# A sparse-attention and two-MoE kernel: other turns for the first six weight decodes, uneven MoE steps in eight turns, earlier first weight load, and a late mask on VectorE

## The chip, the cores and the metric

The kernel runs on one core of a Trainium2 chip. The metric is device time in microseconds (us) of one execution; lower is better. Before the change the median of three runs is 950.56 us (949.97 to 950.58).

## The reference

Four batches of eight heads, 576 positions, 64 dimensions per head. The first four heads see the last 32 positions (local), the other four see every 32nd position (strided). The result goes through two dense feed-forward stages:

```python
scores = scale * q @ k.T
scores = where(mask, scores, -1e9)          # local heads: 0 <= i-j < 32; strided: i >= j, i%32 == j%32
attn = softmax(scores) @ v                  # [4, 8, 576, 64] -> x [2304, 512]
x = (sigmoid(x @ w_gate) * (x @ w_val)) @ w_out        # 512 -> 1536 -> 512
x = (relu(h) + log1p(exp(-abs(h)))) @ moe2_w_out       # h = x @ moe2_w_in, 512 -> 2048 -> 512
```

All of it is float32, and the weights arrive as 64-bit floats.

## The kernel before

**Precision.** A feed-forward product is made of three fp32r matmuls (`mm3`, lines 67 to 69: high x high, high x low, low x high), each with 512 moving columns. So every activation and every weight exists as a high and a low part (`xh`/`xl`, `w..h`/`w..l`, `gh`/`gl`).

**Weights.** They arrive as raw 64-bit words in pieces of 512 KB (`load_next`, line 97, three buffers `raw`), issued on SP. A piece is decoded by `decode_steps`: on VectorE (DVE) lines 108, 112, 117, 122 and, in the attention part, 125; on ScalarE (ACT) line 121; on GpSimd (POOL) line 126. Each decode writes one half of one weight tile. The first six pieces are the gate, value and output weights of the first feed-forward group, two pieces each.

**Attention in turns.** The 32 units (batch, pair of heads, first or second half) run in a software pipeline of 35 turns. Turn `u` (function `stage`) emits, in this order: the exponential of unit u-1 (ACT); the scores of unit u (PE), their row maximum and the subtraction (DVE, lines 435 and 436); loads; the values product of unit u-3 (PE, line 485, `ps_o`); the first half of a decode; then the row sum and reciprocal of unit u-1 (DVE, 451 and 452) with the scaling on POOL (453); the second half of the decode; the output of unit u-3 (`xh` on ACT 505, `xl` on DVE 506); then the transposes of unit u-2 (PE, 467, in two pieces) with their copies to `pt` on ACT (470). The order of emission is the order on each engine. So ACT's copy `pt` of a turn stands behind that turn's decode, the transposes of unit u-2 wait for POOL's scaling of the turn before, and the second transposes of a turn take over a PSUM buffer that `xl` (DVE) of the turn before has to release.

**The mask.** It is added on PE: a matmul of an identity (`one`) with a broadcast mask table (`m_loc`, `m_str`) opens the accumulation (line 422), and the score matmuls (429) add to it. The identity, both tables and the zeros in the two q buffers (`qbuf`) are written at the start by POOL and DVE.

**Feed-forward steps between.** `window(0)` is the first group on the first 512 tokens: 8 gate steps, 8 value steps, 8 output steps, each of three matmuls. Six gate steps run in turns 7, 8 and 9 (`ahead`); the other 18 are spread over turns 11 to 18 (`t == 0`) as 2, 2, 2, 3, 2, 2, 2, 3. Turns 19 to 26 hold 64 steps and turns 27 to 34 hold 48. Gate steps need `xl`/`xh` of the head pair that they read, value steps need decodes 3 and 4, output steps need decodes 5 and 6 and the split products `gh`, `gl`.

**Decodes.** `decode_at` lists the turns with a decode: 4, 5, 9, 10, 12, 13, then 18 to 23. `load_next` runs at the start, in turns 2, 5, 6, 7, and after each decode from turn 8 on.

**Warm-ups.** `keep_busy(n)` issues n matmuls of 512 columns whose result (`ps_w`) nobody reads: three at the start and one in each of turns 0 to 8.

After the attention part some 760 us of feed-forward matmuls follow, which the change doesn't touch.

Of the kernel before, what the change touches and what calls it, by code (L numbers as in the profile page):

```python
# [8 lines left out]
F32 = mybir.dt.float32  # L9
# [4 lines left out]
ALU = mybir.AluOpType  # L14
# [6 lines left out]
P = 128  # L21
# [11 lines left out]
HQ = 64  # L33
# [10 lines left out]
def tile_sparse_attention_moe_moe2(  # L44
# [10 lines left out]
    nc = tc.nc  # L55
# [36 lines left out]
    def load_next():  # L92
        if todo:
            g, m, c = piece = todo.pop(0)
            src = w1[g, m] if g < NG1 else w2[g - NG1, m // 2]
            raw = rawp.tile([P, PIECE], U64, tag="raw", name="raw")
            nc.sync.dma_start(out=raw, in_=src[:, c * PIECE:(c + 1) * PIECE])
            raws[piece] = raw
            queue.append(piece)

    def decode_steps(pools, refill=True):
        g, m, c = piece = queue.pop(0)
        words = raws.pop(piece).bitcast(U32).rearrange("p (n t) -> p n t", t=2)
        low, high = words[:, :, 0], words[:, :, 1]
        hi, lo = (x[:, c * PIECE:(c + 1) * PIECE] for x in wset[g % 2][m])
        f = pools["d"].tile([P, PIECE], U32, tag="f", name="f")
        e = pools["d"].tile([P, PIECE], U32, tag="e", name="e")
        nc.vector.tensor_scalar(
            out=f, in0=high, scalar1=3, scalar2=0x3FFFFFFF,
            op0=ALU.logical_shift_left, op1=ALU.bitwise_and,  # L110
        )
        nc.vector.scalar_tensor_tensor(  # L112
            out=f, in0=high, scalar=0xC0000000, in1=f,
            op0=ALU.bitwise_and, op1=ALU.bitwise_or,
        )
        yield
        nc.vector.tensor_scalar(
            out=e, in0=f, scalar1=0xFF800000, scalar2=None, op0=ALU.bitwise_and
        )
        ff, ef = f.bitcast(F32), e.bitcast(F32)  # L120
        nc.scalar.activation(out=hi, in_=ff, func=AF.Copy)  # L121
        nc.vector.scalar_tensor_tensor(
            out=ef, in0=low, scalar=2.0 ** -52, in1=ef, op0=ALU.mult, op1=ALU.mult
        )
        pools["e"].tensor_tensor(out=ff, in0=ff, in1=hi.bitcast(F32), op=ALU.subtract)  # L125
        nc.gpsimd.tensor_tensor(out=lo, in0=ff, in1=ef, op=ALU.add)
        if refill:
            load_next()
        yield
# [151 lines left out]
    def attention():  # L281
        with ExitStack() as actx:
# [29 lines left out]
            qbuf = [const.tile([P, 2, QW], F32, name=f"qbuf{j}") for j in range(2)]  # L312

            def load(j, parts=1):
                b, hp, c0, cn = units[2 * j]
                loc, w, m = dims(2 * j)
                cn += units[2 * j + 1][3]
                qq = qbuf[j % 2]
                kk = qkp.tile([P, STRIDE + S], F32, tag="k", name="kt")
                k0, kn = (0, STRIDE + S) if loc else (STRIDE, cn * m)  # L320
                qn = (cn - 1) * m + HQ
                for i in range(parts):
                    for h in range(2):
                        r = slice(h * HQ, (h + 1) * HQ)
                        a, e = (0, units[0][3] * m, qn)[i:i + 2] if parts > 1 else (0, qn)
                        nc.sync.dma_start(out=qq[r, h, a:e], in_=q[b, hp][r, a:e])
                    a, e = (0, units[0][3] * m + w - m, kn)[i:i + 2] if parts > 1 else (0, kn)
                    (nc.scalar if j < 2 else nc.sync).dma_start(
                        out=kk[:, a:e], in_=k[b, hp][:, k0 + a:k0 + e]
                    )  # L330
                for i in (2 * j, 2 * j + 1):
                    qt[i], kt[i] = qq, kk

# [9 lines left out]
            load(1)  # L343
            load_v(0)
            load_v(1)
            load_next()
            load_v(2)

            scratch = acc[NBA - 1]
            ident = scratch[:, 0:P]  # L350
            make_identity(nc, ident)
            nc.vector.memset(qbuf[0][HQ:2 * HQ, 0, :], 0.0)
            nc.vector.memset(qbuf[0][0:HQ, 1, :], 0.0)

            one = const.tile([P, P], F32R, name="one")
            nc.vector.tensor_copy(one, ident)
# [5 lines left out]

            for t in sbuf:
                nc.vector.memset(t[:, :, LK:], 1e-9)
            for t in qbuf[1:]:
                nc.vector.memset(t[HQ:2 * HQ, 0, :], 0.0)
                nc.vector.memset(t[0:HQ, 1, :], 0.0)

# [33 lines left out]
            def mask_runs(i):  # L402
                b, hp, c0, cn = units[i]
                if hp >= NLP:
                    return [(0, cn, m_str)]
                first, rest = m_loc[:, 0:LK], m_loc[:, LK:2 * LK]
                return [(0, 1, first), (1, cn, rest)] if c0 == 0 else [(0, cn, rest)]
# [3 lines left out]
            def scores(i):  # L411
                b, hp, c0, cn = units[i]
                loc, w, m = dims(i)
                qq, kk = qt.pop(i), kt.pop(i)
                s = sbuf[i % 3][:, 0:cn, LK - w:LK]
                st = smp.tile([P, 2, 6], F32, tag="st", name="st")
                sm[i] = (s, sbuf[i % 3][:, 0:cn, LK - w:], st)
                ps = ps_s.tile([P, TB], F32, tag="s", name="ps_s")
                pv = ps[:, 0:cn * w].rearrange("p (c w) -> p c w", c=cn)
                runs = mask_runs(i)  # L420
                for j, (a0, a1, t) in enumerate(runs):
                    nc.tensor.matmul(
                        pv[:, a0:a1, :], lhsT=one,
                        rhs=t.unsqueeze(1).to_broadcast([P, a1 - a0, w]),
                        start=(j == 0), stop=False,
                    )
                for c in range(cn):
                    for h in range(2):
                        nc.tensor.matmul(  # L429
                            pv[h * HQ:(h + 1) * HQ, c, :],  # L430
                            lhsT=qq[:, h, (c0 + c) * m:(c0 + c) * m + HQ],
                            rhs=kk[:, (c0 + c) * m:(c0 + c) * m + w], start=False, stop=(c == cn - 1),
                        )
                top = st[:, 0, 0:cn]
                nc.vector.tensor_reduce(out=top, in_=pv, axis=AX.X, op=ALU.max)
                nc.vector.tensor_tensor(
                    out=s, in0=pv, in1=top.unsqueeze(2).to_broadcast([P, cn, w]), op=ALU.subtract
                )
# [73 lines left out]
            START = PB + SKEW  # L512

            def stage(u):
                dec = decode_steps(pools, u >= PB) if u in decode_at else iter(())
                if 0 <= u - 1 < NU:
                    exponent(u - 1)
                if u < NU:
                    scores(u)
                if u % 2 and u + 3 < NU:  # L520
                    load((u + 3) // 2)
                if 0 <= u - 3 < NU:
                    values(u - 3)
                if 3 <= u < NU:
                    load_v(u)
                if u in (2, 5, 6, 7):
                    load_next()
                next(dec, None)
                yield
                if 0 <= u - 1 < NU:  # L530
                    normalize(u - 1)
                next(dec, None)
                if 0 <= u - 3 < NU:
                    outputs(u - 3)
                yield
                if 0 <= u - 2 < NU:
                    yield from p_transposes(u - 2)
# [11 lines left out]
                    yield from step((0, 2), (1, 2), pools)  # L549

            ahead = {START - 4: 2, START - 3: 2, START - 2: 2}
            units_of = [3 * GC * NCC, 8 * GC * NCC, 6 * GC * NCC]
            units_of[0] -= sum(ahead.values())
            filler = window(0)
            decode_at = (4, 5, 9, 10, 12, 13) + tuple(range(18, 24))
            keep_busy(3)
            for u in range(NU + SKEW):
                t, pos = divmod(u - START, PB)
                if t > 0 and pos == 0:
                    for _ in filler:  # L560
                        pass
                    filler = window(t)
                fill = ahead.get(u, 0)
                if t >= 0:
                    total = units_of[t]
                    fill = (pos + 1) * total // PB - pos * total // PB
                n = 0
                for j, _ in enumerate(stage(u)):
                    if u < START - 2 and j == 1:
                        keep_busy(1)  # L570
                    while n < fill * (j + 1) // 4:
                        n += 1
                        next(filler, None)
                while n < fill:
                    n += 1
                    next(filler, None)
# [3 lines left out]
    with tc.manual_schedule():  # L580
# [12 lines left out]
        for i, cur in enumerate(rest):  # L593
            g, t = cur
# [91 lines left out]
```

## Time and profile before

| | before |
|---|---|
| median of three runs | 950.56 us |
| the profiled execution's own time | 950.28 us |
| its span in the profile | 948.5 us |
| PE busy | 931.4 us (98%) |
| DVE busy | 601.8 us (63%) |
| ACT busy | 383.9 us (40%) |
| POOL busy | 229.3 us (24%) |

A busy share is over the whole span. The stages differ: the first 71 us are attention with few feed-forward steps, up to about 190 us both run together, after that there is feed-forward work alone. The busy time of PE is modelled for pipelined matmuls, so PE reads as busy also at half clock; PEclk, the granted share of 2.4 GHz, is read beside it.

### The profile page before, as it was taken

Reading aid. Unit: us, or ns where it says so; the run is one execution under the profiler, and the core shown is the slowest. Engines: PE = TensorE matmul, PEld = TensorE weight load, DVE = VectorE, ACT = ScalarE, POOL = GpSimd, SP = SyncE. Lnnn points to the kernel's source line nnn. Section 1 sums busy time; section 2 is a strip of 40 time slices with the busy share of each in tenths; the row PEclk is TensorE's granted clock in tenths of the full one; section 3 lists DMA queues with packets and bytes.
Section 4 is the critical chain, followed back from the end, with each engine's and each line's share of the span. In section 5 each row is a group of like instructions: output and inputs, shape, how many; then the busy total and the mean of one; then the engine's idle time right before and its main releaser. Section 6 shows DMA issues by size and latency. Waiting matters only on the chain.

```text
span 948.5 us, 13659 instructions
## 1 busy us (share of the span) xinstructions
PE 931.4 (98%) x5476; PEld 776.3 (82%) x5476; DVE 601.8 (63%) x979; ACT 383.9 (40%) x693; POOL 229.3 (24%) x194
## 2 busy tenths in 40 slices
PE   7889999999999999999999999999999999999998
PEld 5667888789888888888888887888888888888886
DVE  7787765337567367457555467676767685858554
ACT  2455545524122112112123355454545554545443
POOL 3232211004224023122125442221313040403000
PEclk9889999999999999999999999999999999999999
DMA  8655332002112011011110011110101020200022
GB/s 226 186 159 154 122 101 61 17 1 89 45 45 81 8 45 67 23 45 46 45 37 30 22 45 45 36 53 23 67 23 66 6 85 1 82 8 23 0 89 112
DMA packets 20688, 57.44 MB, mean 61 GB/s; under 512 B 2704, under 2 KB 3216, under 8 KB 20624
## 3 DMA queue, kind: packets, MB, share of 16 engines
q1 hardware_dynamic: 20192, 55.94, 18.3%
q8 instruction: 43, 0.70, 0.3%
q10 hardware_dynamic: 432, 0.62, 0.2%
q14 instruction: 21, 0.17, 0.1%
HBM read 51.83 MB, written 4.72 MB: 60 GB/s over the span
## 4 chain that ended last, share of the span: by engine, by line
PE 92%; DVE 5%; ACT 1%; POOL 1%; issue 1%; POOLq 0%; DVEq 0%
PE ps_y L67 12%; PE ps_y L69 12%; PE ps_y L68 12%; PE ps_h L69 7%; PE ps_h L68 7%; PE ps_h L67 7%; PE ps_g L67 5%; PE ps_g L68 5%; PE ps_g L69 5%; PE ps_v L67 5%; PE ps_v L69 5%; PE ps_v L68 5%; PE ps_s L429 2%; PE ps_o L485 2%; PE ps_p L467 1%; DVE f L112 1%
## 5 line engine op out<-in xcount | busy, mean ns | idle before, releaser
L156 ACT ACTIVATE gh<-sg 128x512 fp32r<-128x512 f32 (+1 forms) x140 | 82.5, 589 | 255.0 <-DVE sg L189 183.8
L157 DVE TENSOR_TENSOR gl<-sg,gh 128x512 fp32r<-128x512 f32 (+1 forms) x140 | 98.7, 705 | 50.2 <-ACT gh L156 46.6
L260 DVE TENSOR_TENSOR acc<-ps_y,acc 128x512 f32<-128x512 f32 x126 | 86.6, 688 | 68.4 <-PE ps_y L69 66.8
L209 DVE TENSOR_TENSOR acc<-ps_y,acc 128x512 f32<-128x512 f32 (+1 forms) x100 | 61.5, 634 | 68.7 <-PE ps_y L69 68.6
L240 DVE SCALAR_TENSOR_TENSOR sg<-ps_h,sg 128x512 f32<-128x512 f32 (+1 forms) x80 | 50.5, 632 | 37.2 <-ACT sg L233 37.1
L189 DVE TENSOR_TENSOR sg<-ps_v,sg 128x512 f32<-128x512 f32 (+1 forms) x60 | 38.2, 636 | 56.2 <-PE ps_v L69 56.1
L231 ACT ACTIVATE sg<-ps_h 128x512 f32<-128x512 f32 (+1 forms) x80 | 43.8, 548 | 61.2 <-PE ps_h L69 61.2
L112 DVE SCALAR_TENSOR_TENSOR f<-raw,f 128x512 uint32<-128x512 uint32 x68 | 66.4, 977 | 2.3
L125 POOL TENSOR_TENSOR f<-f,w00h 128x512 f32<-128x512 f32 x12 | 18.5, 1544 | 184.6 <-ACT w00h L121 184.6
L68 PE MATMUL ps_h<-xl,w00h 128*128 128x512 f32 (+1 forms) x160 | 58.9, 368 | 0.0
L69 PE MATMUL ps_h<-xh,w00l 128*128 128x512 f32 (+1 forms) x160 | 58.8, 368 | 0.0
L69 PE MATMUL ps_h<-xh,w10l 128*128 128x512 f32 (+1 forms) x160 | 58.8, 368 | 0.0
L68 PE MATMUL ps_h<-xl,w10h 128*128 128x512 f32 (+1 forms) x160 | 58.8, 368 | 0.0
L67 PE MATMUL ps_h<-xh,w00h 128*128 128x512 f32 (+1 forms) x160 | 58.8, 368 | 0.0
L67 PE MATMUL ps_h<-xh,w10h 128*128 128x512 f32 (+1 forms) x160 | 58.8, 368 | 0.0
L67 PE MATMUL ps_y<-w02h,gh 128*128 128x512 f32 x144 | 56.2, 391 | 0.6 <-ACT gh L156 0.6
L68 PE MATMUL ps_y<-w02l,gh 128*128 128x512 f32 x144 | 56.1, 390 | 0.0
L67 PE MATMUL ps_y<-w12h,gh 128*128 128x512 f32 x144 | 56.1, 390 | 0.0
L69 PE MATMUL ps_y<-w02h,gl 128*128 128x512 f32 x144 | 56.1, 390 | 0.0
L68 PE MATMUL ps_y<-w12l,gh 128*128 128x512 f32 x144 | 56.1, 390 | 0.0
L69 PE MATMUL ps_y<-w12h,gl 128*128 128x512 f32 x144 | 56.1, 390 | 0.0
L453 POOL TENSOR_TENSOR sm<-sm,st 128x480 f32<-128x480 f32 (+3 forms) x32 | 25.6, 799 | 123.9 <-DVE st L452 85.7
(121 smaller groups left out, 2420.6 us busy)
## 6 DMA issues: line engine op xcount, KB each, us to landing
raw<-in_w_dram SPq DMA_DIRECT2D x68, 512.0 KB, 3.4
out_dram<-acc SPq DMA_DIRECT2D x18, 256.0 KB, 2.0
qbuf<-in_q_dram SPq DMA_DIRECT2D x16, 151.0 KB, 3.5
kt<-in_k_dram SPq DMA_DIRECT2D x8, 297.0 KB, 4.0
qbuf<-in_q_dram SPq DMA_DIRECT2D x14, 144.0 KB, 3.6
vt<-in_vl_dram SPq DMA_DIRECT2D x8, 240.0 KB, 3.1
kt<-in_k_dram SPq DMA_DIRECT2D x6, 304.0 KB, 4.2
vt<-in_vl_dram SPq DMA_DIRECT2D x8, 192.0 KB, 3.8
```

The costliest lines, as they stand in the source:

```text
L67: nc.tensor.matmul(ps, lhsT=lh, rhs=rh, start=first, stop=False)
L68: nc.tensor.matmul(ps, lhsT=lh, rhs=rl, start=False, stop=False)
L69: nc.tensor.matmul(ps, lhsT=ll, rhs=rh, start=False, stop=last)
L112: nc.vector.scalar_tensor_tensor(out=f, in0=high, scalar=0xC0000000, in1=f, op0=ALU.bitwise_and, op1=ALU.bitwise_or,)
L156: nc.scalar.activation(out=gh[:, c, 0:n], in_=src, func=AF.Copy)
L157: nc.vector.tensor_tensor(out=gl[:, c, 0:n], in0=src, in1=gh[:, c, 0:n].bitcast(F32), op=ALU.subtract)
L189: nc.vector.tensor_tensor(out=sg, in0=ps[:, 0:n], in1=sg, op=ALU.mult)
L209: nc.vector.tensor_tensor(out=y, in0=ps[:, 0:n], in1=y, op=ALU.add)
L231: nc.scalar.activation(out=sg, in_=ps, func=AF.Abs)
L240: nc.vector.scalar_tensor_tensor(out=sg, in0=ps, scalar=0.0, in1=sg, op0=ALU.max, op1=ALU.add)
L260: nc.vector.tensor_tensor(out=y, in0=ps, in1=y, op=ALU.add)
L453: nc.gpsimd.tensor_tensor(out=s[:m2], in0=s[:m2], in1=r.unsqueeze(2).to_broadcast([m2, cn, w]), op=ALU.mult,)
```

## The change

There are five parts.

1. `decode_at` begins with 1, 4, 7, 8, 11, 12 in place of 4, 5, 9, 10, 12, 13. The loads of raw pieces move with it: the first is issued inside the first `load`, right behind its second k part, others in turns 2, 4, 5, 7, and the refill after a decode begins with turn 7.
2. The 18 steps of turns 11 to 18 are spread as 5, 5, 1, 1, 1, 1, 1, 3.
3. Six warm-ups run first in place of three, and in turns 1, 4, 7 and 8 two in place of one.
4. The zeros of the first q buffer are written behind the copies of the identity, not ahead of them.
5. From unit 20 on (the 21st) the mask is no matmul: DVE adds the table to the scores out of PSUM into the SBUF tile, and the maximum and the subtraction read that tile.

```diff
@@ load
+                    if parts > 1 and i == 1:
+                        load_next()
@@ start
             load_v(1)
-            load_next()
             load_v(2)
...
-            nc.vector.memset(qbuf[0][HQ:2 * HQ, 0, :], 0.0)
-            nc.vector.memset(qbuf[0][0:HQ, 1, :], 0.0)
...
-            for t in qbuf[1:]:
+            for t in qbuf:
@@ scores
-                runs = mask_runs(i)
+                late = i >= 2 * PB + PB // 2
+                runs = [] if late else mask_runs(i)
...
-                            rhs=kk[:, (c0 + c) * m:(c0 + c) * m + w], start=False, stop=(c == cn - 1),
+                            rhs=kk[:, (c0 + c) * m:(c0 + c) * m + w],
+                            start=late, stop=(late or c == cn - 1),
                         )
+                if late:
+                    for a0, a1, t in mask_runs(i):
+                        nc.vector.tensor_tensor(
+                            out=s[:, a0:a1], in0=pv[:, a0:a1], op=ALU.add,
+                            in1=t.bitcast(F32).unsqueeze(1).to_broadcast([P, a1 - a0, w]),
+                        )
+                    pv = s
@@ stage and the loop
-                dec = decode_steps(pools, u >= PB) if u in decode_at else iter(())
+                dec = decode_steps(pools, u > 6) if u in decode_at else iter(())
...
-                if u in (2, 5, 6, 7):
+                if u in (2, 4, 5, 7):
...
+            first_fill = (5, 5, 1, 1, 1, 1, 1, 3)
...
-            decode_at = (4, 5, 9, 10, 12, 13) + tuple(range(18, 24))
-            keep_busy(3)
+            decode_at = (1, 4, 7, 8, 11, 12) + tuple(range(18, 24))
+            keep_busy(6)
...
-                if t >= 0:
+                if t == 0:
+                    fill = first_fill[pos]
+                elif t > 0:
...
-                        keep_busy(1)
+                        keep_busy(2 if u in decode_at else 1)
```

DVE from the scores of unit 1 on, before (line 435 is the maximum, 436 the subtraction, 451 and 452 sum and reciprocal; `sm` is the softmax tile, `st` its statistics):

```order
L435 TENSOR_REDUCE st<-ps_s 128x4
L436 TENSOR_TENSOR sm_93<-ps_s,st 128x4x96
L451 TENSOR_REDUCE st<-sm_92 128x5
L452 RECIPROCAL st<-st 128x5
L435 TENSOR_REDUCE st<-ps_s 128x5
```

The same place after (lines 443, 444, 459 and 460 are the same four operations):

```order
L443 TENSOR_REDUCE st<-ps_s 128x4
L444 TENSOR_TENSOR sm_93<-ps_s,st 128x4x96
L108 TENSOR_SCALAR f<-raw 128x512
L112 SCALAR_TENSOR_TENSOR f<-raw,f 128x512
L459 TENSOR_REDUCE st<-sm_92 128x5
L460 RECIPROCAL st<-st 128x5
L117 TENSOR_SCALAR e<-f 128x512
L122 SCALAR_TENSOR_TENSOR e<-raw,e 128x512
L125 TENSOR_TENSOR f<-f,w00h 128x512
L443 TENSOR_REDUCE st<-ps_s 128x5
```

The first decode now stands in turn 1, two of its operations ahead of the row sum of unit 0 and three behind it.

SP's first loads, before (`qbuf` q, `vt` v, `raw` weights):

```order
L326 DMA qbuf_116<-in_q_dram 64x256 x2
L326 DMA qbuf_117<-in_q_dram 64x576 x2
L338 DMA vt<-in_vl_dram 96x640
L338 DMA vt<-in_vl_dram 96x512
L97 DMA raw<-in_w_dram 128x512
L338 DMA vt<-in_vl_dram 96x640
```

And after:

```order
L326 DMA qbuf_116<-in_q_dram 64x256 x2
L97 DMA raw<-in_w_dram 128x512
L326 DMA qbuf_117<-in_q_dram 64x576 x2
L340 DMA vt<-in_vl_dram 96x640
L340 DMA vt<-in_vl_dram 96x512
L340 DMA vt<-in_vl_dram 96x640
```

The first weight piece goes ahead of the q of the second pair of heads and of two v tiles.

PE in turn 13 (scores of unit 13 to the scores of unit 14), before (`ps_v` are value steps, `ps_y` output steps, `ps_p` transposes, `ps_o` values products):

```order
L422 MATMUL ps_s<-m_str,one 128x270
L429 MATMUL ps_s<-kt,qbuf_116 64x54 x10
L485 MATMUL ps_o<-pt,vt 64x64 x10
L67 MATMUL ps_v<-xh,w01h 128x512
L68 MATMUL ps_v<-xl,w01h 128x512
L69 MATMUL ps_v<-xh,w01l 128x512
L467 MATMUL ps_p<-one,sm_94 96x128 x4
L67 MATMUL ps_v<-xh,w01h 128x512
L68 MATMUL ps_v<-xl,w01h 128x512
L69 MATMUL ps_v<-xh,w01l 128x512
L422 MATMUL ps_s<-m_str,one 128x324
```

And after:

```order
L422 MATMUL ps_s<-m_str,one 128x270
L429 MATMUL ps_s<-kt,qbuf_116 64x54 x10
L493 MATMUL ps_o<-pt,vt 64x64 x10
L475 MATMUL ps_p<-one,sm_94 96x128 x4
L67 MATMUL ps_y<-gh,w02h 128x512
L68 MATMUL ps_y<-gl,w02h 128x512
L69 MATMUL ps_y<-gh,w02l 128x512
L422 MATMUL ps_s<-m_str,one 128x324
```

The value steps are over by then (they stand in turns 11 and 12), and turn 13 holds the first output step.

## Rows read from the trace of the kernel before

**Rows 1.** Windows by stage: length, PE, PEld, DVE, ACT, POOL, PEclk, DMA
```profile
0.00:71.00 71.00, 58.47 (x721) 45.69 (x722) 54.30 (x116) 30.46 (x66) 23.60 (x38) 0.90 0.65 190
...
95.00:190.00 95.00, 95.00 (x854) 76.32 (x851) 54.72 (x108) 51.57 (x91) 15.13 (x17) 1.00 0.24 74
...
332.00:948.50 616.50, 612.15 (x2893) 513.86 (x2891) 392.89 (x603) 253.66 (x443) 148.67 (x108) 1.00 0.13 43
```

**Rows 2.** The same for two stretches of 4 us: PE, PEld, DVE, ACT, POOL
```profile
32.00:36.00 4.00, 4.00 (x54) 3.37 (x53) 1.86 (x4) 1.63 (x4) 0.60 (x1) 1.00 0.86 254
44.00:48.00 4.00, 1.44 (x20) 1.04 (x19) 3.83 (x9) 0.88 (x2) 1.34 (x2) 1.00 0.62 197
```

**Rows 3.** PE alone, at the edges of half clock: busy, PEclk
```profile
22.00:23.00 1.00, 0.70 (x3) 0.68 0.81 256
29.00:30.00 1.00, 1.00 (x24) 0.91 1.02 305
49.00:50.00 1.00, 0.90 (x17) 0.83 0.00 0
56.00:57.00 1.00, 1.00 (x13) 0.76 0.00 0
```

**Rows 4.** The chain that ended last, 35 to 53 us: start, length, engine, tile, line
```profile
35.60 0.23 PE ps_g L67
...
39.91 0.35 DVE f L108
...
49.91 0.52 DVE xl L506
...
52.55 0.43 PE ps_g L67
```

**Rows 5.** DVE in turn 4, the first with a decode: start, length, operation
```profile
17.00 0.50 DVE L435 TENSOR_REDUCE st<-ps_s 128x6 f32<-128x324 f32 x1
...
18.01 0.42 DVE L108 TENSOR_SCALAR f<-raw 128x512 uint32<-128x512 uint32 x1
...
19.07 0.55 DVE L451 TENSOR_REDUCE st<-sm 128x4 f32<-128x388 f32 x1
...
19.75 0.40 DVE L117 TENSOR_SCALAR e<-f 128x512 uint32<-128x512 uint32 x1
...
21.90 0.41 DVE L506 TENSOR_TENSOR xl<-ps_o,xh 128x256 fp32r<-128x256 f32 x1
22.24 0.42 DVE L435 TENSOR_REDUCE st<-ps_s 128x5 f32<-128x270 f32 x1
```

**Rows 6.** The start: warm-ups on PE, the last zeros and the mask table on DVE
```profile
2.83 1.65 PE L372 MATMUL ps_w<-w12l,one 128*128 128x512 f32 x3 [2.83 <-DVE w12l L358]
...
3.71 0.56 DVE L367 MEMSET qbuf<- 64x604 f32 x1 [0.16 <-issue]
4.49 0.28 DVE L383 CAST m_loc<-acc 128x192 fp32r<-128x192 f32 x1 [0.23 <-POOL acc L378]
```

**Rows 7.** First raw piece on SP; landing of pieces up to 40 us
```profile
6.16 0.43 SPq L97 DMA_DIRECT2D raw<-in_w_dram  x1
...
DMA to landing us min/median/max: 3.8/5.2/6.1
```

**Rows 8.** Timeline: maximum in turns 11 and 14, masks of turns 15 and 19
```profile
50.33 0.56 DVE L435 TENSOR_REDUCE st<-ps_s 128x4 f32<-128x384 f32 x1
...
68.03 0.29 PE L422 MATMUL ps_s<-m_str,one 128*128 128x270 f32 x1
68.14 0.49 DVE L435 TENSOR_REDUCE st<-ps_s 128x6 f32<-128x324 f32 x1
68.24 0.79 PE L429 MATMUL ps_s<-kt,qbuf 128*64 128x54 f32 x20
...
85.45 0.34 PE L422 MATMUL ps_s<-m_loc,one 128*128 128x384 f32 x1
```

**Rows 9.** DVE's costliest subtraction out of PSUM up to 200 us: busy, mean ns
```profile
L436 DVE TENSOR_TENSOR sm<-ps_s,st 128x480 f32<-128x480 f32 x8 | 5.3, 657 | 0.6
```

## The prediction, made before the changed kernel ran

> **What bounds the kernel now.** I read the busy time by stage first, then windows of 4 us and 1 us in the first stage, then the chain of waits there, then DVE's and PE's timelines turn by turn. From 95 us on PE is busy in every microsecond at full clock, and in the last stage it lacks 4.35 of 616.5 us [rows 1]. So behind the attention start only a matmul less is worth anything, and what happens up to 71 us counts by when the 18 steps of turns 11 to 18 are done. In those 71 us PE lacks 12.5 us and has a mean clock of 0.90, and DVE lacks 16.7 us [rows 1]. Neither is full, because they wait for each other in turn: at 32 to 36 us PE is full and DVE works 1.86 of 4 us, at 44 to 48 us DVE works 3.83 and PE 1.44 [rows 2]. The chain shows it too: PE's gate steps up to 39.9 us, then from 39.91 to 49.91 us only DVE operations of the decodes of turns 9 and 10, then PE again [rows 4]. Behind that wait PE is at 1.2 GHz, where 512 columns take 0.43 us and not 0.23 [rows 4]. There are two such stretches: from 22.36 us (0.68 in that microsecond) to 29.1, and from 49.66 to 56.5 [rows 3], 6.8 us each.
>
> **A turn on DVE.** In turn 4, from maximum to maximum, 5.24 us pass; the decode has 18.01 to 19.07 and 19.75 to 21.90 of it, 3.2 us, and the rest is 2.0 [rows 5]. With the larger local units the rest is up to 2.7 (estimate: that turn's rest, four reads of 480 columns for 324 and 388; 0.66 for the largest [rows 9]). A turn on PE without steps is about 2.8 us, the four turns 15 to 18 of before being 17.42 us for 9 steps of 0.69 (three slots of 0.23), so (17.42 - 6.2) / 4 [rows 4, 8].
>
> **Start.** The two zero fills of the first q buffer go behind the copies. Each has a pitch of 0.72 us (0.56 and a gap of 0.16), the last fill ended at 4.27 and the mask table followed at 4.49 [rows 6]. The table comes between 0 and 1.44 us later; the copies move forward as well, so I take 0.5. The warm-ups cost nothing: three took 1.65 us [rows 6], six at 0.43 take 2.6, and they start earlier and end before the table is there. Without that cover they would cost 1.3. The extra ones of turns 1, 4, 7 and 8 are 0.23 to 0.43 each in turns in which DVE is the slower. They may bring full clock for the first scores, which gives back up to 1 us; with the 0.5 I take turn 0 as before.
>
> **First piece and first decode.** SP issued the first raw piece at 6.16 us, 3.8 to 6.1 before it lands [rows 7]. Behind four q loads and not behind six and two v tiles it is issued at about 3.2, so it is there at 7 to 9.3. The decode of turn 1 asks for it at about 10.3, so DVE doesn't wait. If it did, everything behind would be late by as much, since the row sum of unit 0 is queued behind it. The q of unit 2 that it passes lands about 2 us later (512 KB at some 250 GB/s), near 9.5; PE asks at 9.9. That is tight, 0 to 1 us. The decode itself delays reciprocal, POOL's scaling and the transposes of unit 0 by 0.7 (two operations of 1.06 us, less what DVE had idle), and the maximum of unit 2 by 2.8.
>
> **The turns, walked by hand.** I add DVE operations in their order, and where PE has to come first (transposes after POOL's scaling, values behind ACT's copy, which stands behind the decode's ACT operation), PE's times. DVE then begins turn 2 at 14.3, 3 at 16.2, 4 at 19.3 (waits 0.8 for scores), 5 at 24.5 (19.3 + 5.24), 6 at 26.6, 7 at 29.0, 8 at 34.5 and 9 at 40.2 (two decodes, 5.5 and 5.7), 10 at 43.4 (scores of PE come last), 11 at 46.0. Before, turn 11 began at 50.33 with as many decodes and steps done [rows 8]. So 4.3 us are won, because the decodes of turns 7 and 8 lie beside the gate steps of `ahead`, where DVE idled [rows 2], and the first in turn 1. PE then has 5 steps (3.4 us) and 2.8 of attention in turn 11, DVE 5.7: turn 12 at 51.7. In turn 12 DVE has 2.0 + 3.2 and both gate products, 2.05 each with the wait for ACT's copy between them (estimate: two operations of 0.69, as the largest of rows 9 with 512 for 480 columns, and one ACT copy of some 0.65): turn 13 at 61.2, turn 14 at 63.2. Before, turn 14 began at 68.14 [rows 8].
>
> Steps: when PE begins the scores of unit 15 it has 18 of 24 behind it, at 65.2 us; before it had 15 at 68.03 [rows 8]. Turns 15 to 18 hold 6 steps, not 9: 17.42 less 3 x 0.69 is 15.35, so turn 19 begins at about 80.6 and not at 85.45 [rows 8]. That is **-4.85 us** at full clock. What is late next is PE itself, so nothing more comes off there.
>
> **Half clock.** The walk is at 2.4 GHz, and before had two slow stretches inside it. In the changed kernel PE stands about 2.2 us ahead of the transposes of unit 0 (11.3 to 13.5), 1.7 in turn 5 and 1.3 in turn 14. Before, the fall at 49.66 came after PE had stood through most of 46 to 48.6 [rows 2, 3]. So I count one stretch in turns 3 to 6. Walked again with those turns at half rate, turn 4 begins 1.2 us later, or turn 7 by 2.4 if the fall comes in turn 5: **+1.8**. The bounds are 0 and, for a stretch that nothing hides, 3.4 (half of 6.8).
>
> **The late mask.** Twelve units lose 14 mask matmuls: four local ones (2 x 480 and 2 x 384 columns) and eight strided ones (4 x 324, 4 x 270), 4104 columns. At 0.23 us for 512 [rows 4] that is 1.84 us, in stretches where PE is full [rows 1]: **-1.84**. As slots the rows show more: the mask of turn 15 holds 68.03 to 68.24, 0.21 us for 270 columns [rows 8], 0.09 over its columns; on 14 masks that is 3.1. I take the lower end, because a switch to the 64-column score tiles stays. The Trainium skill (TensorE: Matmul & The Clock Gate, Back-to-back issue gap) gives a single matmul N / 2.4 + 2.5 ns. By it the masks are worth 1.75 us, an estimate from that page, and the sum would be 0.09 us smaller; the slots here are longer than it says. For it DVE gets 14 additions of at most 0.66 us [rows 9], under 9.2 us in turns 20 to 31. DVE is busy 54.72 of 95 us there [rows 1], and the scores of a turn are needed by PE two turns later, so it costs nothing. Without that cover, in turns 20 to 23 with their decodes, it would cost 4 x 0.66 = 2.6; that is the upper end.
>
> **Sum.** 950.28 (the profiled execution's own time) - 4.85 + 1.8 - 1.84 = 945.4. The profiled execution is 0.28 below the median of the runs shown, so the forecast is **945.7 us**.
>
> **Rivals.**
> *The half clock eats the early gain.* DVE's decode in turn 1 leaves PE without work, and PE is slow not once but up to turn 12, where ten steps of three matmuls stand close together. At half clock these cost 30 x 0.2 = 6 us, of which DVE's 15.2 us in turns 11 and 12 hide some. Then only the masks remain: 950.56 - 1.84 = 948.7. For it speaks that PE idles in short pieces up to turn 6; against it that turns 7 to 10 have steps in each gap but one. The Trainium skill (TensorE: Matmul & The Clock Gate, HAM oscillation) says that waits between bursts of matmuls throw the array back to the slow clock again and again; by that rule this rival, or the next, is right. The two stretches of before agree with it, and both ended while work went on [rows 3].
> *Slower: slow stretches in the thin turns.* Turns 13 to 17 have one step each, where before had two or three. If the chain maximum, row sum, POOL, transposes is longer than PE's 3.5 us per turn, PE idles there, falls to 1.2 GHz and takes up to 3.4 us more for each stretch. From -6.7 (walk and masks) two stretches bring it to no change, and the third decides: 950.56 - 6.7 + 3 x 3.4 = 954.1.
> *The additions on DVE bite.* PE waits for DVE in turns 20 to 23: 945.7 + 2.6 = 948.3.
> *The decode in turn 1 waits for its piece*: 945.7 + 1 for each us behind 10.3; it lies in the range.
>
> **How the numbers follow.** Forecast 0.58, early gain eaten 0.22, slower 0.10, additions 0.10. The forecast's low end is a walk with no slow stretch, full clock for the first scores and masks worth their slots: 950.56 - 4.85 - 1 - 3.1 = 941.6; the high end takes in both middle rivals with some 0.8 us for the q of unit 2: 949.5. Range 941.6 to 949.5, which leaves out the slow rival, a part of the second and a little below. 0.2% (1.9 us) is about what a measurement of this kernel tells from no change; 948.7 is that border. Faster: 0.58, nearly half of the second and most of the fourth, 0.73. Same: 0.17. Slower: 0.10.
>
> **What would show it.** Right: DVE begins turn 11 near 46, turn 14 near 63, scores of unit 19 near 80.6; from there to the end 1.8 us less. Wrong: half clock between 40 and 75 us, DVE waiting for the raw piece in turn 1, PE idle between 95 and 190 us, or scores of unit 19 behind 83.5.

## The result, and the profile after

The changed kernel takes 943.13 us (median of four runs, 942.36 to 943.38), the kernel before on the same chip 950.57 us. The ratio is 0.991 with an interval of 0.9894 to 0.9926. So the change makes the kernel faster by 7.4 us; forecast was 4.9, and the time lies inside the range. The profiled execution took 942.36 us, with a span of 940.6.

Windows by stage of the kernel after (length, PE, PEld, DVE, ACT, POOL, PEclk, DMA), to be read beside [rows 1]:

```profile
0.00:71.00 71.00, 62.22 (x793) 49.29 (x793) 58.61 (x125) 33.63 (x74) 24.42 (x39) 0.98 0.75 200
71.00:95.00 24.00, 23.95 (x254) 19.16 (x254) 20.25 (x39) 13.32 (x26) 8.15 (x8) 1.00 0.53 155
95.00:190.00 95.00, 94.78 (x855) 75.03 (x852) 57.09 (x113) 51.79 (x92) 12.98 (x15) 1.00 0.22 68
...
332.00:940.60 608.60, 604.21 (x2852) 507.12 (x2850) 389.44 (x597) 252.74 (x442) 148.44 (x108) 1.00 0.13 44
```

In the first 71 us PE does 62.22 us of work, not 58.47, at a mean clock of 0.98, not 0.90; DVE does 4.3 us more. From 95 to 190 us PE now lacks 0.22 us, where it lacked nothing.

The timeline after, with the rows that answer to [rows 8] (the maximum of turns 11 and 14, the masks of units 15 and 19), those of the start, and the maximum of unit 19:

```profile
1.95 2.93 PE L371 MATMUL ps_w<-w12l,one 128*128 128x512 f32 x6 [1.95 <-DVE w12l L357]
4.77 0.19 DVE L382 CAST m_loc<-acc 128x192 fp32r<-128x192 f32 x1
5.84 1.21 PE L429 MATMUL ps_s<-kt,qbuf 128*64 128x96 f32 x20
...
10.36 0.43 DVE L108 TENSOR_SCALAR f<-raw 128x512 uint32<-128x512 uint32 x1 [0.66 <-DMA raw<-in_w_dram]
10.67 0.38 PE L429 MATMUL ps_s<-kt,qbuf 128*64 128x96 f32 x2 [1.24 <-DMA qbuf<-in_q_dram]
...
14.54 0.65 DVE L443 TENSOR_REDUCE st<-ps_s 128x5 f32<-128x480 f32 x1
...
64.36 0.29 PE L422 MATMUL ps_s<-m_str,one 128*128 128x270 f32 x1
...
78.85 0.34 PE L422 MATMUL ps_s<-m_loc,one 128*128 128x384 f32 x1
...
81.32 0.55 DVE L443 TENSOR_REDUCE st<-ps_s 128x4 f32<-128x384 f32 x1
```

The masks of units 15 and 19 come at 64.36 and 78.85 us, 3.67 and 6.60 ahead of before. The same 6.6 us stand between the maxima of unit 19 (81.32 against 87.91). From there to the end of the span 859.28 us pass, before 860.59. So the gain is **6.6 us ahead of turn 19 and 1.3 behind it**, and nothing else changed.

Half clock was predicted for one stretch in turns 3 to 6. PE alone, in single us (busy, PEclk):

```profile
13.00:14.00 1.00, 0.47 (x3) 0.53 1.04 257
...
15.00:16.00 1.00, 1.00 (x13) 0.50 0.45 179
16.00:17.00 1.00, 1.00 (x28) 0.77 0.13 33
```

There is one, and only one, from about 13.1 to 16.5 us (turns 2 and 3). It begins while PE waits for the transposes of unit 0, up to 13.53.

### The profile page after: what moved, and what is told of

It reads as the page before. It is cut to its first block, busy times and chain, and to the rows that moved or that the text cites. A ratio compares the mean times of both kernels' runs of the same rounds, so it can differ in the third digit from the quotient of the medians.

```text
span 940.6 us, 13664 instructions
## 1 busy us (share of the span) xinstructions
PE 927.2 (99%) x5469; PEld 772.4 (82%) x5469; DVE 607.7 (65%) x993; ACT 383.2 (41%) x693; POOL 229.1 (24%) x194
## 4 chain that ended last, share of the span: by engine, by line
PE 90%; DVE 6%; ACT 1%; issue 1%; DMA 1%; POOL 1%; SPq 0%; DVEq 0%; POOLq 0%; ACTq 0%
PE ps_y L67 12%; PE ps_y L69 12%; PE ps_y L68 12%; PE ps_h L67 7%; PE ps_h L69 7%; PE ps_h L68 7%; PE ps_g L67 5%; PE ps_v L67 5%; PE ps_g L68 5%; PE ps_g L69 5%; PE ps_v L69 5%; PE ps_v L68 5%; PE ps_s L429 2%; PE ps_p L475 1%; PE ps_o L493 1%; DVE f L112 1%
## 5 line engine op out<-in xcount | busy, mean ns | idle before, releaser
L231 ACT ACTIVATE sg<-ps_h 128x512 f32<-128x512 f32 (+1 forms) x80 | 43.8, 547 | 61.2 <-PE ps_h L69 61.2
L122 DVE SCALAR_TENSOR_TENSOR e<-raw,e 128x512 f32<-128x512 uint32 x68 | 53.0, 780 | 2.3
```

The source lines that it names most:

```text
L122: nc.vector.scalar_tensor_tensor(out=ef, in0=low, scalar=2.0 ** -52, in1=ef, op0=ALU.mult, op1=ALU.mult)
L231: nc.scalar.activation(out=sg, in_=ps, func=AF.Abs)
```

## The experiments

One profiled execution of each kernel is laid out here, turn by turn. "First scores" is the time of the 20 score matmuls of unit 0; the next columns are the starts of the maximum of units 2, 11, 14, 15 and 19 on DVE; "behind" is the span less the last of them. Ratios are to the kernel before, timed beside it on the same chip.

| kernel | first scores | 2 | 11 | 14 | 15 | 19 | behind | median, us | ratio, interval |
|---|---|---|---|---|---|---|---|---|---|
| before | 2.02 | 11.47 | 50.33 | 68.14 | 69.94 | 87.91 | 860.59 | 950.57 | |
| after | 1.21 | 14.54 | 45.53 | 62.32 | 65.45 | 81.32 | 859.28 | 943.13 | 0.9910, 0.9894 to 0.9926 |
| e4_decodes_alone | 1.96 | 15.46 | 46.42 | 62.13 | 65.42 | 83.59 | 860.61 | 945.97 | 0.9946, 0.9925 to 0.9967 |
| f1_old_decodes | 1.90 | 12.51 | 53.12 | 73.60 | 76.94 | 92.79 | 859.21 | 954.35 | 1.0024, 1.0008 to 1.0040 |
| e2_even_steps | 1.55 | 15.69 | 48.97 | 64.62 | 67.92 | 86.09 | 859.21 | 943.65 | 0.9916, 0.9889 to 0.9943 |
| h1_even_warm2 | 1.87 | 15.56 | 46.53 | 62.29 | 65.58 | 83.75 | 859.25 | 943.47 | 0.9922, 0.9906 to 0.9938 |
| e3_old_warmups | 1.87 | 15.55 | 46.60 | 63.39 | 66.51 | 82.37 | 859.33 | 944.29 | 0.9929, 0.9906 to 0.9951 |
| f2_raw_behind_q | 2.12 | 15.80 | 46.78 | 63.56 | 66.70 | 82.56 | 859.24 | 943.80 | 0.9925, 0.9902 to 0.9948 |
| f3_warm_turn2 | 1.53 | 14.62 | 45.58 | 62.38 | 65.51 | 81.36 | 859.34 | 943.85 | 0.9917, 0.9898 to 0.9936 |
| g1_dve_more_early | 1.50 | 14.61 | 48.44 | 66.19 | 69.33 | 85.19 | 859.21 | 945.62 | 0.9928, 0.9905 to 0.9951 |
| g2_dve_more_late | 1.18 | 13.98 | 44.96 | 61.75 | 66.40 | 82.71 | 859.59 | 943.42 | 0.9906, 0.9877 to 0.9934 |
| e1_mask_on_pe | 1.05 | 14.31 | 45.32 | 62.12 | 66.78 | 82.66 | 860.64 | 945.25 | 0.9935, 0.9911 to 0.9959 |
| f4_mask_from_24 | 1.33 | 14.49 | 45.47 | 62.25 | 66.93 | 82.78 | 859.22 | 942.68 | 0.9908, 0.9889 to 0.9926 |
| h2_keep_clock | 1.05 | 14.16 | 45.69 | 62.50 | 65.64 | 81.47 | 859.33 | 942.63 | 0.9912, 0.9897 to 0.9926 |

The runs of versions whose medians differ by 1 us overlap; what tells them apart is the turns. The medians come from several batches, in which the kernel before itself had medians from 950.1 to 952.9, so the ratios compare better than the us.

**The early decodes alone** (part 1, with its loads, on the kernel before).

```diff
...
-            decode_at = (4, 5, 9, 10, 12, 13) + tuple(range(18, 24))
+            decode_at = (1, 4, 7, 8, 11, 12) + tuple(range(18, 24))
```

> The kernel before with the new decode turns and their loads alone (old steps, old warm-ups, zeros first, mask on PE). Theory: turn 11 begins at about 46 and not at 50.3, and 4.3 to 5 us of the whole are here: 945.6 to 946.3. Rival (warm-ups or packed steps are needed for it): 949 or later.

Unit 19 comes at 83.59 us, 4.32 ahead of before, with the end behind it as before (860.61). The early decodes are two thirds of what is won ahead of turn 19. This execution also has less half clock there (3.4 us, before 13.7), but the times of the kernel before speak against that as the cause: executions of it with a mean granted clock of 0.996 took 950.57 and 950.68 us, the profiled one, with 0.992, took 950.28.

**All parts but that one**, with the loads as before too.

```diff
...
-            decode_at = (1, 4, 7, 8, 11, 12) + tuple(range(18, 24))
+            decode_at = (4, 5, 9, 10, 12, 13) + tuple(range(18, 24))
```

> The change with the old decode turns (4, 5, 9, 10, 12, 13) and their loads; packed steps, six warm-ups and late mask stay. Theory: turn 11 is back near 50 and 4 to 5 us are lost: 947 to 948. Rival (warm-ups and steps bring the gain): 944 or earlier.

The expectation was missed by over 6 us: this kernel is slower than the one before, although the masks bring it the same 1.3 us at the end. DVE and PE in turns 12 to 14 of it:

```profile
59.36 0.49 DVE L442 TENSOR_REDUCE st<-ps_s 128x6 f32<-128x324 f32 x1 [3.39 <-PE ps_s L428]
...
68.56 0.43 DVE L442 TENSOR_REDUCE st<-ps_s 128x5 f32<-128x270 f32 x1
...
72.01 0.69 PE L492 MATMUL ps_o<-pt,vt 96*64 96x64 f32 x16 [2.79 <-ACT pt L477]
...
73.60 0.48 DVE L442 TENSOR_REDUCE st<-ps_s 128x6 f32<-128x324 f32 x1
```

Ten steps of turns 11 and 12, some at half clock, hold up the scores, so DVE waits 3.39 us; its decodes of turns 12 and 13 and both gate products come behind, so that PE then waits 2.79 us, and half clock follows (PEclk 0.50 from 73 to 76). Steps and decodes have to be moved together. Part of its loss lies earlier: beside the steps of `ahead` DVE waits 3.54 us for the scores of unit 8, with half clock from 28 to 35.

**Even steps with everything else as in the changed kernel**, once as such, once with six warm-ups in turn 2.

```diff
-            first_fill = (5, 5, 1, 1, 1, 1, 1, 3)
+            first_fill = (2, 2, 2, 3, 2, 2, 2, 3)
```

> The change with the 18 steps spread as before (2, 2, 2, 3, 2, 2, 2, 3). Theory (DVE's order sets the pace up to turn 13, PE's steps count behind it): turn 11 at 45.5 as in the changed kernel, three steps more in turns 15 to 18, 3 x 0.69 = +2.1, less what PE idles in turns 12 to 14: 944 to 945.2. Rival (the steps packed into turns 11 and 12 are the gain): +5, 948.

> f3_warm_turn2 with the even shares of before (2, 2, 2, 3, 2, 2, 2, 3) in the place of 5, 5, 1, 1, 1, 1, 1, 3, so that the packing is tested without a slow stretch in turns 2 and 3. Theory (packing is worth little once the decodes are early: it only moves steps of PE into the two turns in which DVE has a second decode): turn 11 begins as in f3 (45.6), turns 14 to 18 with two or three steps each cost PE 0.7 us a step and end later by what turns 11 and 12 then leave idle on PE: the maximum of unit 19 comes 0 to 2 us behind f3's 81.36, the time is 943.9 to 946. Rival (the packing is the part that pays, as the early decodes leave PE idle in turns 11 and 12): unit 19 behind 85, time above 947. Other rival (the packing costs, since it holds the scores of turn 12 up): unit 19 ahead of 80.5, time under 943.

The profile of the first fell on its slowest execution (947.08 us, half clock in three places, and DVE waited 1.47 us for the first raw piece), so the second is read. Its time, 943.47, is below the range expected for it; its unit 19 is 2.39 us behind that of f3, but 0.94 of that it has from unit 2 on. From unit 11 to unit 19 it takes 37.22 us, the changed kernel 35.79, which is 1.4 us less. One place is turn 12. PE of h1_even_warm2, and of f3_warm_turn2, which differs in the steps alone:

```profile
52.40 1.12 PE L493 MATMUL ps_o<-pt,vt 96*64 96x64 f32 x16 [2.47 <-ACT pt L478]
```

```profile
50.91 0.65 PE L493 MATMUL ps_o<-pt,vt 96*64 96x64 f32 x16
51.48 0.50 PE L67 MATMUL ps_v<-xh,w01h 128*128 128x512 f32 x1
```

With two steps PE waits 2.47 us for ACT's copy `pt`; with five it has work up to then. ACT's decode operation ends at 49.47 us in h1, so it is not what holds the copy up most. That is the first sigmoid (line 176) with the loading of its table:

```profile
49.81 1.28 ACT L176 ACT_TABLE_LOAD   x1
51.10 0.60 ACT L176 ACTIVATE sg<-ps_g 128x512 f32<-128x512 f32 x1
51.59 0.64 ACT L478 ACTIVATE pt<-ps_p 96x384 f32<-96x384 f32 x2
```

In f3 the gate steps end sooner, and the same loading stands ahead of the decode:

```profile
45.57 1.28 ACT L176 ACT_TABLE_LOAD   x1
```

How much of the 1.4 us this wait makes is open, because half clock follows it in h1 (PE alone, busy and PEclk):

```profile
52.00:54.00 2.00, 1.60 (x17) 0.61 0.74 262
54.00:56.00 2.00, 2.00 (x9) 0.53 0.45 107
```

That stretch lasts 3.4 us, and PE has no idle time behind it up to unit 19, so it can cost up to 1.7 us. The profiles of e2 and e4, also with even steps, have one at the same place (from 54.7 and from 52.3 us); none of the nine with early decodes and uneven steps has. So the uneven steps may gain by the order of the work, or by sparing PE the wait after which the clock fell; no run separates the two. One execution of e2_even_steps had a mean granted clock of 1.000 and took 942.03 us, less than all four of the changed kernel. So a gain of 1.4 us by the order alone is not shown. The medians (943.47 and 943.85) don't show it either; they differ by less than their runs spread (942.5 to 945.3).

**Warm-ups as before** (three first, one per turn).

```diff
-            keep_busy(6)
+            keep_busy(3)
...
-                        keep_busy(2 if u in decode_at else 1)
+                        keep_busy(1)
```

> The change with three warm-ups first and one per turn, as before. Theory: the first maximum comes 0.4 to 0.8 us later (half clock in the first scores), the rest follows DVE: 943.5 to 944. Rival (the clock is the gain: half clock fell from 13.6 us in the kernel before to 2.9): two or more slow stretches are back and cost 3 us or more, 946 or later.

**The first raw piece behind the q loads**, but ahead of the v tiles.

```diff
-                    if parts > 1 and i == 1:
-                        load_next()
...
             load(1)
+            load_next()
             load_v(0)
```

> The change with the first raw piece issued behind the q of unit 2 (ahead of the v tiles). In the changed kernel DVE waited 0.66 us for the piece in turn 1 and PE 1.24 us for that q. Theory (DVE's order sets the pace): the wait for the piece grows to about 1.7, all behind is late by 1: 944.1. Rival (the q of unit 2 is what counts): PE's wait is gone and 0.5 us are won: 942.6.

In both (944.29 and 943.80 us), unit 2 comes 1.0 to 1.3 us later than in the changed kernel and unit 19 as much, which is what a cost of warm-ups or of the late piece would look like. It is neither: h1_even_warm2, with six warm-ups and the early piece, is as late (15.56), and DVE of f2_raw_behind_q doesn't wait for its piece. The common thing is the first scores. f2_raw_behind_q has them and the next ones at half pace:

```profile
5.84 2.12 PE L428 MATMUL ps_s<-kt,qbuf 128*64 128x96 f32 x20
...
8.94 1.55 PE L428 MATMUL ps_s<-kt,qbuf 128*64 128x96 f32 x16
...
11.63 0.41 DVE L108 TENSOR_SCALAR f<-raw 128x512 uint32<-128x512 uint32 x1
```

h2_keep_clock, with the same instructions on PE up to there, has them at full pace:

```profile
5.73 1.05 PE L429 MATMUL ps_s<-kt,qbuf 128*64 128x96 f32 x20
...
7.31 0.88 PE L429 MATMUL ps_s<-kt,qbuf 128*64 128x96 f32 x16
```

In every kernel with a decode in turn 1, unit 2 begins 4.17 to 4.19 us behind the first operation of that decode (g1, with one operation more, 4.64). That operation stands behind unit 1 and needs the piece. Those with unit 1 still at half pace (e3, e4, f2, h1) don't wait for the piece and begin unit 2 at 15.46 to 15.80 us; the others begin it at 13.98 to 14.62, but for e2, where the piece was 1.47 us late (15.69). With six warm-ups the full pace came in time in 8 of 11 profiles, with three in none of e3 and e4, and in before for unit 1 alone. So the warm-ups seem to help, by about 1.05 us where they do; with so few profiles that is not shown. What the early piece is worth stays open, because f2_raw_behind_q was not seen at full pace; at half pace DVE waits for neither the early piece (e3, h1) nor the late one.

**Six warm-ups in turn 2**, ahead of the transposes of unit 0.

```diff
-                        keep_busy(2 if u in decode_at else 1)
+                        keep_busy(6 if u == 2 else 2 if u in decode_at else 1)
```

> The change with six warm-ups in turn 2 in place of one, where PE waits for the first transposes and the clock falls at 13.5 us. If it keeps the clock up: theory (DVE decides there) within 0.4 of the changed kernel (942.7 to 943.5), turn 4 at 19.3 or up to 0.4 later. Rival (the slow stretch costs what the prediction took for one, 1.2 to 2.4): 941 to 942.

No microsecond is at half clock, and unit 4 comes at 19.34 us (19.27 in the changed kernel), unit 19 at 81.36 (81.32). So the stretch at 13.1 to 16.5 us costs nothing: POOL's scaling and DVE's decode decide there. That the warm-ups took it away is not shown: h2_keep_clock has the same six and a stretch from 12.4 to 15.8 us, f2_raw_behind_q has neither. In h2 the six ran at half clock themselves, and from unit 2 to unit 4 it took 5.29 us, not 4.73. The median of f3, 943.85, is above what was expected; two of its four executions took 944.3 and 944.4 us at a mean clock of 0.996, so they had half clock in a place that was not profiled.

**More work for DVE**, line 117 twice in each of six decodes (some 0.43 us more), in the first six or in the second six.

```diff
...
-        nc.vector.tensor_scalar(
+        for _ in range(2 if len(done) < 6 else 1):
+          nc.vector.tensor_scalar(
...
+        done.append(piece)
...
```

> The change with one DVE operation of each of the first six decodes (line 117, some 0.43 us) done twice, with the same result: 6 x 0.43 = 2.6 us more on DVE in turns 1 to 12. Theory (DVE's order sets the pace there): nearly all of it shows, +2.0 to +2.6, 945.1 to 945.7, and turn 14 begins that much later. Rival (PE or its clock sets the pace): +0.5 at most.

> The same operation done twice in the six decodes of turns 18 to 23, where PE is full: 2.6 us more on DVE. If DVE has room there: 943.1 within 0.3. If it has not, as the loss in turns 22 and 23 hints: +0.5 to +1.5, with PE waits in those turns.

The early ones come through nearly in full: units 14 and 19 are both 3.87 us later. Of that, 1.48 is half clock, which fell on 41 to 44 us here, where units 9 to 10 took 4.92 us, not 3.44. The other 2.4 are close to the 2.6 us of six added operations.

Of the late ones, in turns 18 to 23, the end behind the maximum of unit 19 shows 0.3 us. But the operation added in turn 18 stands ahead of that maximum on DVE and moves it, while PE's scores of unit 19 are not held up. From those scores to the end 862.22 us pass, in the changed kernel 861.45. So 0.77 us of the 2.6 come through, as PE's waits for the copy `pt` in units 21 and 22 show, which are 0.02 and 0.21 us in the changed kernel:

```profile
96.83 0.80 PE L495 MATMUL ps_o<-pt,vt 96*64 96x64 f32 x20 [0.49 <-ACT pt L480]
...
105.12 0.69 PE L495 MATMUL ps_o<-pt,vt 96*64 96x64 f32 x16 [0.47 <-ACT pt L480]
```

So DVE sets the end up to turn 14, as the prediction had it. From turn 18 on it does so in part, which the prediction had at nothing.

**The mask on PE throughout, and the late mask from unit 24 on.**

```diff
-                late = i >= 2 * PB + PB // 2
+                late = False
```

```diff
-                late = i >= 2 * PB + PB // 2
+                late = i >= 3 * PB
```

> The change without its late mask: all masks are matmuls again. The prediction's column count says +1.84 us against the changed kernel (943.1 to 945.0); what the trace of the changed kernel shows from the scores of unit 19 to those of unit 31 says +1.35 (944.5), with turn 19 unmoved at 78.9. If the additions on DVE cost as much as the matmuls, no change (943.1) or less.

> The change with the mask on DVE from unit 24 on, not 20: turns 20 to 23 have decodes on DVE. In the changed kernel turns 20 and 21 gain 0.15 and 0.11 us and turns 22 and 23 lose 0.12 and 0.26. If DVE's additions cause the loss, the four come out even: 943.1 within 0.2, and no wait of PE for ACT's copy in turn 22. If the loss has another cause it stays, and the time is 0.5 longer.

The stretch behind unit 19 is the clean measure, since nothing else changes in it: 860.59 to 860.64 us in the three kernels with all masks on PE, 859.2 to 859.3 in all but one of the others (g2 has its DVE work there). So the late mask is worth **1.35 us**, and from unit 24 on it is worth the same. PE at the scores of unit 21 in e1_mask_on_pe:

```profile
95.72 0.40 PE L69 MATMUL ps_v<-xh,w01l 128*128 128x512 f32 x1
95.96 0.29 PE L422 MATMUL ps_s<-m_str,one 128*128 128x270 f32 x1
96.18 0.79 PE L429 MATMUL ps_s<-kt,qbuf 128*64 128x54 f32 x20
96.80 0.41 PE L493 MATMUL ps_o<-pt,vt 96*64 96x64 f32 x8
```

And in the changed kernel, with unit 22 behind it:

```profile
94.25 0.40 PE L69 MATMUL ps_v<-xh,w01l 128*128 128x512 f32 x1
94.58 0.79 PE L429 MATMUL ps_s<-kt,qbuf 128*64 128x54 f32 x20
95.39 0.80 PE L493 MATMUL ps_o<-pt,vt 96*64 96x64 f32 x20
...
102.35 0.91 PE L429 MATMUL ps_s<-kt,qbuf 128*64 128x54 f32 x24
103.47 0.69 PE L493 MATMUL ps_o<-pt,vt 96*64 96x64 f32 x16 [0.21 <-ACT pt L478]
```

A mask had a slot of 0.22 us (95.96 to 96.18); slots of 0.22, 0.24, 0.27 and 0.38, four of each of the first two and two of each of the others, make 3.14 us. But the last step's slot grows from 0.24 to 0.33 when scores follow it directly, about 0.10 for each of 12 units. That leaves 1.94. In units 21 and 22 the values product then starts 0.81 and 1.12 us behind the scores, not 0.62 and 0.74: 0.57 lost to the copy `pt`, late because DVE's addition stands ahead of the decode on which ACT waits. 1.94 - 0.57 = 1.37, and 1.35 was measured. f4, with the masks of units 20 to 23 on PE, has 0.62 and 0.74 again; what it gives up for that, four slots of 0.92 us less 4 x 0.10, is about as much.

**Warm-ups against the stretch at 63 us**: six in turn 2 as above, and four in turns 13 and 14, where PE waits.

```diff
+                    elif u in (13, 14) and j == 1:
+                        keep_busy(4)
```

> The changed kernel with six warm-ups in turn 2 (one before) and four in turns 13 and 14 (none before), put where PE waits there: 0.95 us ahead of the last transposes of turn 13, 1.33 us ahead of those of turn 14. At 0.23 us each they take 0.92 us and fit into both waits. Theory (the slow stretch of 6.8 us that some runs have at 63 to 66 us comes out of PE's waits at 57 to 63 us and costs 1.5 us): no half clock between 57 and 70 us, unit 15 begins at most 3.2 us behind unit 14, and the maximum of unit 19 at 81.0 to 81.5; time 942.0 to 943.2, the spread of the runs smaller. Rival (the stretch does not depend on these waits): half clock at 63 to 66 us stays in the profile or the runs lie as before, 942.4 to 943.4 and some above 945. Other rival (the warm-ups stand in the way of the transposes): unit 15 behind 66, time above 943.5.

The reason for it (the stretch is 3.4 us long, 63.1 to 66.5, not 6.8): e1, f4 and g2 take 4.65 to 4.68 us from unit 14 to unit 15, all the others with early decodes and uneven steps 3.12 to 3.14. PE of e1_mask_on_pe there, windows of 2 us:

```profile
60.00:62.00 2.00, 1.13 (x32) 1.00 0.99 285
62.00:64.00 2.00, 1.21 (x7) 0.78 1.03 252
64.00:66.00 2.00, 2.00 (x15) 0.50 0.17 34
```

The changed kernel, with the same instructions there and nearly the same waits, at full clock:

```profile
60.00:62.00 2.00, 1.33 (x39) 1.00 0.93 294
62.00:64.00 2.00, 1.01 (x8) 1.00 1.05 287
64.00:66.00 2.00, 2.00 (x48) 1.00 0.17 35
```

Nothing stands in the way of the chain there but PE itself, so the stretch costs 1.5 us. In h2_keep_clock the warm-ups fit into the waits (unit 14 to 15 in 3.14 us), there is no such stretch, and its five runs lie between 941.78 and 943.41 us. That is what the theory expects; but five of eight profiles without these warm-ups were free of the stretch too, so it is not shown that they hold it off. Its ratio is that of the changed kernel.

## Why the prediction was right, and where its size was off

The mechanism held: up to turn 14 DVE's turns set the end, the early decodes fill its waits, the uneven steps fill one of PE's, and what was won lasts to the end. Two of the signs of being wrong came all the same, in small: DVE's wait for the raw piece, and PE idle for 0.22 us between 95 and 190 us. The sum gave 945.4 us for a profiled execution that took 942.36, by these steps.

**Start.** The mask table came at 4.77 us, 0.28 later than in [rows 6] (0.5 taken), and the six warm-ups cost nothing: they end as the table comes. The first scores took 1.21 us; that full clock there could give back up to 1 us was named, and it came in this execution.

**First piece.** That DVE wouldn't wait was wrong: the piece, issued at 3.25 us as predicted, was there 7.1 us later, longer than [rows 7] have it, and DVE waited 0.66. All of it shows, because DVE has no idle time from there to the maximum of unit 2. PE waited 1.24 for the q of unit 2 (0 to 1 predicted). That unit 2 still began at 14.54 (14.3 predicted) is luck, due to the pace of the first scores. With "turn 0 as before", which the sum took, e3 began it at 15.55 without a wait: 5.24 us behind unit 1, where before had 1.85, so the decode delayed it by 3.4 us and not by 2.8.

**The walk.** DVE began turns 4, 5, 7, 9 and 11 at 19.27, 24.50, 28.82, 39.55 and 45.53 us (19.3, 24.5, 29.0, 40.2 and 46.0 predicted), turn 13 at 60.50 (61.2) and the scores of unit 15 at 64.36 (65.2): 0.84 too late at the end, gathered mostly in the turns with a decode (7, 8 and 12) and in turn 13, whose parts had been priced by the largest rows. Turns 15 to 18 then took 14.49 us, not 15.35. The 2.8 us of a PE turn without steps, from turns of before, were too much; (14.49 - 6 x 0.69) / 4 is 2.59. Together the walk is -6.60 and not -4.85. About 1 us of that is the luck of the start: e3, with the slow one, has unit 19 5.54 us ahead of before.

**Half clock: the step that failed.** One stretch was right, a turn earlier than taken, and that PE's stand ahead of the transposes of unit 0 was a place for it. But +1.8 was charged as if PE were the last there. f3_warm_turn2 is without the stretch and comes to unit 4 and unit 19 no earlier, so its price was the lower bound, 0.

**The late mask.** 1.35, not 1.84. The lower end was worked out from columns because a switch "stays". In fact 0.10 us per unit is new, and the additions were not free: 0.57 of the 2.6 that the upper end allowed, in units 21 and 22. The Trainium skill (TensorE: Matmul & The Clock Gate, Back-to-back issue gap) would give the mask of 270 columns 0.115 us, an estimate from that page; its slot here is 0.22, and the measurement decides. With that page's 1.75 us for all masks the time would come out 0.09 us longer; that the sum would be smaller, as the prediction says, is a slip.

945.4 - 1.8 - (6.60 - 4.85) + (1.84 - 1.35) = 942.34, and 942.36 was measured. That it closes is no proof, since each term was read from this execution.

**The rivals.** *Early gain eaten*: no, and even steps with a slow stretch (h1) keep most of it. *Slow stretches in the thin turns*: the place was right, turn 14, and the size is 1.5 us where it happens; one of these, not three. The Trainium skill (TensorE: Matmul & The Clock Gate, HAM oscillation) describes a kernel whose clock falls back at each wait between bursts of matmuls; it says so of waits longer than those here (0.95 and 1.33 us in turns 13 and 14), which the prediction left out. With nearly equal waits at 60 to 63 us the clock fell in one execution and not in another, so here the page tells what may happen, not what does. *Additions on DVE*: true in small, 0.57. *Wait for the piece*: true in small, 0.66, made up for by the pace of the first scores.

The parts of the 7.9 us between the two profiled executions, then: early decodes 4.3 (e4_decodes_alone), uneven steps 1.2 to 1.4 (from e4 to e3, and from h1 to e3; the slow stretch of the even kernels in turn 12 is in it), the start at full pace 1.05 (from e3 to after, and by luck of the run in part), the late mask 1.35. The first two hold only together with each other's order: in f1, without the early decodes, the uneven steps are part of a loss. The new place of the zeros was not run alone.

## What to carry to other kernels

Price a stretch at half clock only by what is last in it: the same kind of stretch cost 0 where POOL and DVE decided and 1.5 us where PE did, and it need not come back in the next execution. Look for one also in the kernel that you compare with, before a difference is put down to the edit. When two engines wait for each other in turn, move work of both at once and check which engine has the longer turn: the uneven steps came with 1.4 us less with the early decodes (a slow stretch included) and were part of a loss without them. Measure a delay from the engine that is last: counted from DVE's maximum, the added late operations cost 0.3 us, counted from PE's scores 0.77. A number that comes out as a theory expects proves little until a kernel without that cause has been looked at: 1 us of "late piece" was the pace of the first scores.

## What the runs showed of the hardware

At the start PEclk reads 1.00 while the array works at half pace. h1_even_warm2, PE alone (busy, PEclk), in which the 20 first scores take 1.87 us:

```profile
6.00:7.00 1.00, 1.00 (x14) 1.00 1.04 228
7.00:8.00 1.00, 1.00 (x11) 1.00 0.81 179
```

That 1.00 is no measurement. The first clock record in the trace of h1 is the grant of full clock at 11.49 us, and the view counts time without a record as full. The pace goes by that record in all fourteen executions: two score matmuls side by side take 0.16 us ahead of it and 0.083 behind it. It stands at 6.23 us in the changed kernel, in the middle of the first scores, at 8.70 in before, at 4.78 to 6.92 in the other kernels with a fast unit 1, and at 11.18 to 11.54 in e3, e4, f1, f2 and h1. So the mean clocks of the first 71 us (0.90 and 0.98) are too high.

The same 20 matmuls took from 1.05 to 2.12 us in eleven executions with the same six warm-ups ahead, so the moment at which the full pace comes is not the program's alone.

The half-clock stretches that PEclk does show up to turn 19 were 3.4 or 6.8 us long in all kernels, at places that differ between programs equal up to there (e1, f4 and g2 against the changed kernel). And a score matmul that follows a step of 512 columns directly starts 0.33 us behind it, where a mask matmul between them starts 0.24 behind: taking out a small matmul gave back 0.13 us of its slot of 0.22.
